# Folding the k and q weights in 64 x 64 tiles, and a stated order of landings for the first loads

## The chip, the cores and the metric

The kernel runs on one core of a Trainium2 chip. The time is device time in microseconds (us) of the whole program; smaller is better. The instructions of a core go to five engines that each work through a queue of their own, in order: TensorE (PE in the profile; its weight loads are shown apart as PEld), VectorE (DVE), ScalarE (ACT), GpSimd (POOL) and SyncE (SP), which here only issues DMA transfers. An engine that has to wait for another one waits on a semaphore, and everything behind the waiting instruction in its queue waits with it.

## The reference

One transformer block on x of 2048 tokens by 640 features, with adaptive layer norm from a condition vector c:

```python
mod = (_silu(c) @ w_mod).reshape(c.shape[0], 6, 1, -1)
sa, ca, ga, sb, cb, gb = (mod[:, 0], mod[:, 1], ...)
h = _layernorm(x, axis=-1) * (1 + ca) + sa
x = x + ga * _A_ref(h, A_wqkv, A_w_phi, A_wo)
h = _layernorm(x, axis=-1) * (1 + cb) + sb
x = x + gb * _B_ref(h, B_w1, B_b1, B_w2, B_b2)
```

`_A_ref` is linear attention with 32 heads of 20 features. Each head's q and k go through that head's own 20 x 20 matrix before two softmaxes:

```python
pq = jnp.einsum("bhsd,hdf->bhsf", q, w_phi)
pk = jnp.einsum("bhsd,hdf->bhsf", k, w_phi)
phi_q = jnp.concatenate([_softmax(pq, axis=-1), _softmax(-pq, axis=-1)], axis=-1)
```

`_B_ref` is an MLP with a squared ReLU. The change touches only the work that comes before the first projection of tokens: `w_phi` is multiplied into the q and k weights once (the folds), the first 256 tokens are normalised, and shift `sa` and scale `ca` are computed from c.

## The kernel before

**Stages.** The kernel has a prologue (lines 149 to 691 of the source below), a loop over 16 blocks of 128 tokens for k, v, q and the attention sums, a second pass that makes the attention output, and the MLP. In the prologue the order of each engine's instructions is the order of the source (`tc.manual_schedule` at line 150 names all five engines).

**The folds.** `fold(nm, d)` at line 265 makes 128 rows (chunk d, of five) of the k or q weights with `w_phi` multiplied in. The raw weights lie transposed: 120 columns, or six heads, on 120 partitions, five such groups side by side in one chunk, and the last 40 columns of all chunks in a small piece of their own (`wk1`, `wq1`). The moving operand `bd_t` is block diagonal: six 20 x 20 blocks of `w_phi` for each group (lines 241 to 251, from the loaded `bd` and the mask `own`). So one fold is six products of 120 x 128 weights with 120 (the last: 40) moving columns, into two PSUM banks. In fp32 a product is two records in the profile, so a fold has 12 records. Then `split()` copies each bank to SBUF, rounded, with ACT and puts the rest beside it with DVE (`lo`, line 91). `pj` is a set of four PSUM banks, so two folds can be under way; the first fold of q uses two of the three `kvp` banks instead.

**The other work of the prologue.** `stats` (line 543) takes mean and variance of the first 256 tokens with DVE and then makes bias and scale of the norm with four small POOL instructions (lines 553 to 556). `scale` (line 559) applies them with ACT. `t_in` (line 354) turns the normalised block with PE, ten transposes into `TR`, halves of the `kvp` banks. `mod_rows2` (line 568) multiplies c into a chunk of the shift and scale weights (`WM`, loaded from `w_ss`), with four 32-column tiles side by side; `mod_sb` copies the result to SBUF with ACT, `mod_cols2` turns it with PE and sums it with DVE into `cols_a`. `out0(d)` applies `cols_a` to chunk d of the turned tokens with ACT twice and DVE once (`t_out`, line 365). `k_step(d)` is the first use of all this: 12 products of the k projection.

**The order on PE** is written out in lines 614 to 655: nine warm-up products, the folds of k's chunks 0 to 3, then of k's chunk 4 and q's chunks 0 to 3, the first `mod_rows2`, the transposes of x, and after them a chain of columns, second `mod_rows2`, q's last fold, third `mod_rows2`, and the five `k_step`. On ACT `scale` stands between the splits of q's chunks 1 and 2; on DVE `stats` stands between the splits of k's chunks 3 and 4.

**The loads.** SP issues them in the order of lines 226 to 239: k's five chunks and small piece, the first block of x, q's chunks 0 to 3, two chunks of `w_ss`, q's chunk 4, the other three of `w_ss`, the second block of x, v's five chunks. A load waits only for its destination, and for the landing of the transfer issued eight before it, whose semaphore it uses again. POOL sets up constants and masks at the start (lines 153 to 199).

Of the kernel before, what the change touches and what calls it, by code (L numbers as in the profile page):

```python
# [11 lines left out]
AF = mybir.ActivationFunctionType  # L12
ALU = mybir.AluOpType
# [41 lines left out]
def kernel(  # L55
# [34 lines left out]
    def lo(out_lo, full, hi, eng=None):  # L90
        (eng or nc.vector).tensor_tensor(out_lo, full, hi.bitcast(F32), op=ALU.subtract)  # L91
# [4 lines left out]
    def over(ap):  # L96
        return ap[:, :, None].to_broadcast([ap.shape[0], ap.shape[1], DH])
# [43 lines left out]
    def tp(name):  # L141
# [17 lines left out]
    nc.gpsimd.affine_select(out=own, in_=own, compare_op=ALU.is_ge, fill=0.0, base=0,  # L159
                            pattern=[[-DH, 6]], channel_multiplier=1)  # L160
    nc.gpsimd.affine_select(out=own, in_=own, compare_op=ALU.is_ge, fill=0.0, base=DH - 1,
                            pattern=[[DH, 6]], channel_multiplier=-1)
# [20 lines left out]
    for v in vt:  # L183
        nc.gpsimd.memset(v[:, :, DH :], 1.0)

    def head_mask(m, n, at):

        nc.gpsimd.memset(m, 1.0)
        nc.gpsimd.affine_select(out=m, in_=m, compare_op=ALU.is_ge, fill=0.0, base=-at,
                                pattern=[[-DH, n]], channel_multiplier=1)  # L190
        nc.gpsimd.affine_select(out=m, in_=m, compare_op=ALU.is_ge, fill=0.0, base=DH - 1 + at,
                                pattern=[[DH, n]], channel_multiplier=-1)

    mtmp = row("s2", "mtmp")
    mask = mask[:, :3]
    for m, t, n in ((mask, mtmp[:120, :3], 3), (mask5, mtmp[:80, :2], 2)):
        head_mask(m, n, 0)
        head_mask(t, n, DH * n)
        nc.gpsimd.tensor_tensor(m, m, t, op=ALU.add)

    nc.scalar.dma_start(bdc[:120, :120], bd)
    nc.scalar.dma_start(c_t, c)
    bd_t = row("s4", "bd_t")
    raw, WM, RV, XB = {}, {}, {}, {}

    def load_raw(nm, w5, w1, ds=range(NC)):
        if 0 in ds:
            raw[nm] = [tok2("w", f"raw_{nm}{i}") for i in range(3)]
            nc.vector.memset(raw[nm][2][:, 1], 0.0)
        for d in ds:  # L210
            nc.sync.dma_start(raw[nm][d // 2][:, d % 2], w5[d * P : (d + 1) * P])
            if d == 0:
                nc.sync.dma_start(raw[nm][2][:40, 1], w1)

    def load_x(j):
        XB[j] = tok2(f"x{j % 2}", f"xb{j}")
        nc.sync.dma_start(XB[j], x[256 * j : 256 * j + 256].rearrange("(i p) d -> p i d", p=P))

    def load_wm(d):
        WM[d] = flat(tok2(("k", "k", "q0", "q1", "w")[d], f"wm_{d}"))  # L220
        nc.sync.dma_start(WM[d], w_ss[d * P : (d + 1) * P])

    def flat(e):
        return e.rearrange("p s d -> p (s d)")

    load_raw("k", wk5, wk1)
    load_x(0)
    load_raw("q", wq5, wq1, range(4))
    for d in range(2):
        load_wm(d)  # L230
    load_raw("q", wq5, wq1, (4,))
    for d in range(2, NC):
        load_wm(d)
    load_x(1)
    for d in range(NC):
        if d % 2 == 0:
            both = tok2("w", f"rawv{d}")
        RV[d] = both[:, d % 2]
        nc.sync.dma_start(RV[d], wv[d * P : (d + 1) * P])

    by_head = bdc[:120, :120].rearrange("p (g f) -> p g f", f=DH)
    for a, b in ((0, 3), (3, 5)):
        nc.vector.tensor_tensor(
            bd_t[:120, 120 * a : 120 * b].rearrange("p (g i f) -> p g i f", i=6, f=DH),
            by_head[:, a:b, None, :].to_broadcast([120, b - a, 6, DH]),
            own[:, None, :, None].to_broadcast([120, b - a, 6, DH]), op=ALU.mult
        )
    nc.vector.tensor_tensor(
        bd_t[:120, 600:].rearrange("p (i f) -> p i f", f=DH),
        by_head[:, 5:6, :].to_broadcast([120, 2, DH]), over(own[:, :2]), op=ALU.mult  # L250
    )

    cs = const.tile([P, NC], F32, name="cs")
# [11 lines left out]
    def fold(nm, d, p=None):  # L265

        w = wslot(f"w{nm}{d}")
        W[nm, d] = w
        p = p or pj(f"fold{nm}{d}")
        for g, (o, n) in enumerate(GR):  # L270
            if g < 5:
                r = raw[nm][d // 2][:120, d % 2, g * P : (g + 1) * P]
            else:
                r = raw[nm][2][:120, 1, d * P : (d + 1) * P]
            nc.tensor.matmul(  # L275
                p[g // 3][:, (g % 3) * 120 : (g % 3) * 120 + n], r, bd_t[:120, g * 120 : g * 120 + n],
                start=True, stop=True,
            )

        def split():  # L280
            for h, (a, b) in enumerate(((0, 360), (360, 640))):
                nc.scalar.activation(w[:, 0, a:b], p[h][:, : b - a], AF.Copy)
                lo(w[:, 1, a:b], p[h][:, : b - a], w[:, 0, a:b])

        return split

# [67 lines left out]
    def t_in(xn, d, p, mixed=False):  # L354
        for i in range(2):
            src = by_turn(xn[:, i])[:, d] if mixed else xn[:, i, d * P : (d + 1) * P]
            nc.tensor.transpose(p[:, i * P : (i + 1) * P], src, ident)  # L357
# [254 lines left out]
        t_out(cols_a, HT[0], d, "a0", TR[d])  # L612

    warm = tp("warm")
    for i in range(WARM):
        nc.tensor.matmul(warm[:, :P], ones, ones, start=True, stop=True)
    for d in range(4):
        fold("k", d)()
    n0 = stats(XB[0], "a0")
    fold("k", 4)()  # L620
    fold("q", 0, kvp[1:])()
    fold("q", 1)()
    scale(XB[0], *n0)
    fold("q", 2)()
    split = fold("q", 3)
    mod_rows2(0)
    mod_sb(0)
    for d in range(NC):
        t_in(XB[0], d, TR[d])
    split()  # L630
    mod_cols2(0)
    out0(0)
    mod_rows2(1)
# [21 lines left out]

    def v_hi(d):
        W["v", d] = wslot(f"wv{d}")
# [1131 lines left out]
```

## Time and profile before

| | us |
|---|---|
| median of three runs | 747.2 |
| lowest, highest | 746.77, 747.63 |
| the profiled execution, its own time | 746.64 |
| its span, from the first to the last instruction | 744.9 |
| PE busy in the span | 738.1 |
| POOL busy in the span | 169.1 |

The granted TensorE clock is 1.0 in the profiled execution. Busy time says how long an engine had work under way, and not whether the work was of use; the chain of waits follows the end of the program back, at each step to what released it. The rows of the prologue stand in the prediction below, where they are used.

### The profile page before, as it was taken

The numbers are of one execution on the slowest core, as the hardware profiler recorded it, in microseconds if no ns is written. First come the engines' busy times: TensorE is split into PE (matmuls) and PEld (weight loads), VectorE is DVE, ScalarE is ACT, GpSimd is POOL, SyncE is SP. The second block draws the span as 40 slices with busy tenths as digits, with TensorE's granted clock in tenths as the row PEclk, the third lists the DMA queues.
The fourth block names the chain that finished last, engine by engine and source line by source line (L and its number), as shares of the span: only waits on it lengthen the run. The fifth ranks groups of instructions, "written<-read, shape, count | busy, mean of one in ns | idle before, by whom it ended". The sixth has DMA issues, their size and how long they took to land.

```text
span 744.9 us, 16612 instructions
## 1 busy us (share of the span) xinstructions
PE 738.1 (99%) x6523; PEld 720.6 (97%) x6523; DVE 598.8 (80%) x1089; ACT 453.1 (61%) x1028; POOL 169.1 (23%) x352
## 2 busy tenths in 40 slices
PE   9999999999999999999999999999999999999997
PEld 9999999999999988998999999999999999999997
DVE  6598988987999999999755777877786776777766
ACT  5767566657863355567687667475574747647431
POOL 2000101001100337547303040231321313222110
PEclk9999999999999999999999999999999999999999
DMA  8812341343331254754885567897667768667461
GB/s 330 339 37 106 111 134 59 107 143 107 126 124 72 83 184 152 173 137 106 209 251 166 154 199 255 271 312 211 180 190 201 214 184 240 187 176 213 129 183 36
DMA packets 58800, 126.46 MB, mean 170 GB/s; under 512 B 7438, under 2 KB 16403, under 8 KB 58723
## 3 DMA queue, kind: packets, MB, share of 16 engines
q1 hardware_dynamic: 38636, 79.20, 32.4%
q0 software_dynamic: 17504, 40.90, 22.1%
q10 hardware_dynamic: 2583, 5.30, 1.9%
q8 instruction: 51, 0.84, 0.5%
q14 instruction: 26, 0.21, 0.1%
HBM read 100.74 MB, written 29.89 MB: 175 GB/s over the span
## 4 chain that ended last, share of the span: by engine, by line
PE 88%; DVE 6%; ACT 3%; POOL 1%; issue 1%; ACTq 0%; DVEq 0%; POOLq 0%
PE up L81 25%; PE acc L81 18%; PE pk L81 8%; PE pwo L81 8%; PE pv L81 8%; PE pq L81 6%; PE acc3x L81 5%; PE te L943 2%; PE kvp L448 1%; DVE dn L875 1%; PE foldk L275 1%; PE numa L81 1%; PE ta L357 1%; DVE scr L873 1%; PE foldq L275 1%
## 5 line engine op out<-in xcount | busy, mean ns | idle before, releaser
L81 PE MATMUL up<-h,w 128*128 128x256 f32 x1640 | 204.6, 276 | 0.1
L81 PEld LDWEIGHTS up<-h,w 128*128 128x128 f32 x1640 | 196.5, 188 | 0.7 <-DVE h L91 0.5
L1338 ACT ACTIVATE ft<-up,b_t 128x256 f32<-128x256 f32 x104 | 49.2, 473 | 95.6 <-PE up L81 95.2
L81 PE MATMUL acc<-w,ra 128*128 128x384 f32 x452 | 97.5, 335 | 0.0
L1339 DVE TENSOR_TENSOR ft<-ft 128x256 f32<-128x256 f32 x104 | 43.8, 421 | 43.0 <-ACT ft L1338 41.5
L81 PE MATMUL pwo<-wo,ot 128*128 128x384 f32 (+1 forms) x480 | 78.1, 313 | 0.0
L81 PE MATMUL pq<-wq,hT 128*128 128x384 f32 (+1 forms) x480 | 75.8, 312 | 0.0
L81 PEld LDWEIGHTS acc<-w,ra 128*128 128x128 f32 x452 | 72.7, 188 | 0.8 <-DVE ra L91 0.6
L81 PE MATMUL pk<-wk,hT 128*128 128x384 f32 (+1 forms) x480 | 73.1, 309 | 0.0
L81 PE MATMUL pv<-wv,hT 128*128 128x380 f32 (+1 forms) x480 | 73.0, 309 | 0.0
L81 PEld LDWEIGHTS pwo<-wo,ot 128*128 128x128 f32 x480 | 69.5, 188 | 2.8 <-issue 2.7
L81 PEld LDWEIGHTS pq<-wq,hT 128*128 128x128 f32 x480 | 71.3, 188 | 0.7 <-issue 0.5
L81 PEld LDWEIGHTS pv<-wv,hT 128*128 128x128 f32 x480 | 71.3, 188 | 0.0
L81 PEld LDWEIGHTS pk<-wk,hT 128*128 128x128 f32 x480 | 70.8, 188 | 0.5 <-ACT hT L369 0.2
L91 DVE TENSOR_TENSOR ra<-ft,ra 128x384 fp32r<-128x384 f32 (+2 forms) x86 | 36.8, 448 | 32.6 <-ACT ra L1362 18.8
L1448 POOL DMA_DIRECT2D ring_a<-td_a x34 | 18.5, 543 | 117.2 <-PE acc L81 103.5
L1362 ACT ACTIVATE ra<-ft 128x384 fp32r<-128x384 f32 x48 | 25.2, 526 | 28.4 <-DVE ft L1339 22.3
L81 PE MATMUL acc3x<-w,ra 128*128 128x256 f32 x231 | 39.5, 278 | 0.0
L81 PEld LDWEIGHTS acc3x<-w,ra 128*128 128x128 f32 x231 | 37.2, 188 | 0.0
L439 DVE TENSOR_REDUCE sk<-ek 128x64 f32<-128x1280 f32 x16 | 23.7, 1482 | 15.1 <-ACT ek L434 10.7
L1353 DVE TENSOR_TENSOR ft<-ft 128x128 f32<-128x128 f32 x136 | 33.3, 286 | 1.2
L334 POOL TENSOR_SCALAR sma<-sma 128x2 f32<-128x2 f32 x6 | 3.1, 516 | 134.9 <-ACT xb L333 134.9
(255 smaller groups left out, 1442.5 us busy)
## 6 DMA issues: line engine op xcount, KB each, us to landing
ring_c<-td_c POOLq DMA_DIRECT2D x34, 384.0 KB, 4.0
ring_a<-td_a POOLq DMA_DIRECT2D x34, 384.0 KB, 3.4
ring_b<-td_b POOLq DMA_DIRECT2D x34, 256.0 KB, 3.6
esp<-eq SPq DMA_DIRECT2D x12, 640.0 KB
el<-esp SPq DMA_DIRECT2D x12, 640.0 KB
rw<-in_w SPq DMA_DIRECT2D x23, 320.0 KB
wm<-in_w_mod SPq DMA_DIRECT2D x20, 320.0 KB
xb<-in_x SPq DMA_DIRECT2D x8, 640.0 KB
```

What stands on the lines that cost most here:

```text
L81: nc.tensor.matmul(o, a, b, start=first and i == 0, stop=last and i == len(terms) - 1, skip_group_check=skip,)
L91: (eng or nc.vector).tensor_tensor(out_lo, full, hi.bitcast(F32), op=ALU.subtract)
L275: nc.tensor.matmul(p[g // 3][:, (g % 3) * 120 : (g % 3) * 120 + n], r, bd_t[:120, g * 120 : g * 120 + n], start=True, stop=True,)
L357: nc.tensor.transpose(p[:, i * P : (i + 1) * P], src, ident)
L439: nc.vector.tensor_reduce(s, heads(flat(e)), axis=AX.X, op=ALU.add)
L448: nc.tensor.matmul(kvp[0][32 * c : 32 * c + DH + 1, a - g % 3 * DH : a - g % 3 * DH + 2 * m].rearrange("p (s n) -> p s n", s=2)[:, :, h % ...
L943: nc.tensor.transpose(p[:124, a : a + P], EU[2 * j + i][:, 2 * g + c, :124], ident)
L1338: nc.scalar.activation(r, p, AF.Relu, bias=b1_t[:, f : f + 1])
L1339: nc.vector.tensor_tensor(r, r, r, op=ALU.mult)
L1353: nc.vector.tensor_tensor(t[:, o], t[:, a], t[:, b], op=op)
L1362: nc.scalar.activation(a[:, 0, :3], t[:, :3], AF.Copy)
L1448: nc.gpsimd.dma_start(RING[j, n, r], TD[n][r].bitcast(F32R))
```

## The change

It has four parts.

1. **The folds.** Columns of the raw weights are dealt to two halves of the partitions: the first 16 heads to partitions 0 to 59, the other 16 to 64 to 123, 60 columns (three heads) a group, five groups, and the last 20 columns of each half in the small piece. A fold is then six groups of four products, each of a 64 x 64 tile of the raw weights with 60 (the last: 20) moving columns. The two row halves go to the two PSUM banks, the two column halves to the two halves of a bank's partitions. `bd` and `own` follow (the mask of three heads for each half), `bd_t` is made by one DVE instruction, and the splits are cut at 320 columns instead of 360.
2. **The loads.** `load` can be given the landed tile of another load. Then POOL copies one element of that tile into the first element of the destination, and SP's issue waits for the copy. The loads after k's wait so: x's first block for k's chunk 1, q's chunks 0 and 1 for k's chunks 3 and 4, and so on, as written below. Their order on SP is the same. The small pieces are loaded as two halves each. The last nine loads are written behind `stats`, in `loads1()`.
3. **The order.** q's chunk 3 is split before the first `mod_rows2`, and the transposes of x stand before that `mod_rows2`, not behind it. The constant columns of `vt` and the masks are made on POOL after `scale` of the second block.
4. **The warm-up** has three products with 384 moving columns in place of nine with 128.

```diff
+FOLDS = [(60 * g, 60) for g in range(5)] + [(300, DH)]
...
-    own = bdc[:120, P : P + 6]
-    nc.gpsimd.memset(own, 1.0)
...
+    own6 = bdc[:, 120:126]
+    own = own6[:, :3]
+    nc.gpsimd.memset(own6, 1.0)
...
+    nc.gpsimd.tensor_tensor(own, own, own6[:, 3:], op=ALU.add)
...
-    for m, t, n in ((mask, mtmp[:120, :3], 3), (mask5, mtmp[:80, :2], 2)):
-        head_mask(m, n, 0)
-        head_mask(t, n, DH * n)
-        nc.gpsimd.tensor_tensor(m, m, t, op=ALU.add)
...
+    def masks():
+        for v in vt:
+            nc.gpsimd.memset(v[:, :, DH :], 1.0)
+        for m, t, n in ((mask, mtmp[:120, :3], 3), (mask5, mtmp[:80, :2], 2)):
+            head_mask(m, n, 0)
+            head_mask(t, n, DH * n)
+            nc.gpsimd.tensor_tensor(m, m, t, op=ALU.add)
...
+    def head(ap):
+        return ap[:1, :1]
+
+    def load(to, of, after=None):
+        if after is not None:
+            nc.gpsimd.tensor_copy(head(to if len(to.shape) == 2 else to[:, 0]), head(after))
+        nc.sync.dma_start(to, of)
...
+    for d in range(NC):
+        load_raw("k", wk5, wk1, d)
+    k_, q_ = (lambda d: chunk("k", d)), (lambda d: chunk("q", d))
+    load_x(0, k_(1))
+    load_raw("q", wq5, wq1, 0, k_(3))
+    load_raw("q", wq5, wq1, 1, k_(4))
+    load_raw("q", wq5, wq1, 2, XB[0][:, 0])
+    load_raw("q", wq5, wq1, 3, XB[0][:, 0])
+    load_wm(0, q_(0))
+    load_wm(1, q_(2))
+    load_raw("q", wq5, wq1, 4, q_(3))
+
+    def loads1():
+        load_wm(2, WM[0])
+        load_wm(3, WM[1])
+        load_wm(4, q_(4))
+        load_x(1, WM[2])
+        load_v(0, WM[3])
+        load_v(1, WM[4])
+        load_v(2, XB[1][:, 0])
+        load_v(3, XB[1][:, 0])
+        load_v(4, RV[0])
...
-        for g, (o, n) in enumerate(GR):
-            if g < 5:
-                r = raw[nm][d // 2][:120, d % 2, g * P : (g + 1) * P]
-            else:
-                r = raw[nm][2][:120, 1, d * P : (d + 1) * P]
-            nc.tensor.matmul(
-                p[g // 3][:, (g % 3) * 120 : (g % 3) * 120 + n], r, bd_t[:120, g * 120 : g * 120 + n],
-                start=True, stop=True,
-            )
+        for g, (o, n) in enumerate(FOLDS):
+            r = raw[nm][d // 2][:, d % 2, g * P : (g + 1) * P] if g < 5 else raw[nm][2][:, 1, d * P : (d + 1) * P]
+            for a in (0, 64):
+                for c in (0, 64):
+                    nc.tensor.matmul(
+                        p[a // 64][c : c + 64, o : o + n], r[a : a + 64, c : c + 64], bd_t[a : a + 64, o : o + n],
+                        start=(g == 0), stop=True, skip_group_check=True,
+                    )
...
-    for i in range(WARM):
-        nc.tensor.matmul(warm[:, :P], ones, ones, start=True, stop=True)
+    for i in range(WARM // 3):
+        nc.tensor.matmul(warm[:, : 3 * P].rearrange("p (a n) -> p a n", a=3), ones, ones[:, None, :].to_broadcast([P, 3, P]), start=True, stop=True)
     for d in range(4):
         fold("k", d)()
     n0 = stats(XB[0], "a0")
+    loads1()
     fold("k", 4)()
     fold("q", 0, kvp[1:])()
     fold("q", 1)()
     scale(XB[0], *n0)
     fold("q", 2)()
-    split = fold("q", 3)
+    fold("q", 3)()
+    for d in range(NC):
+        t_in(XB[0], d, TR[d])
     mod_rows2(0)
     mod_sb(0)
-    for d in range(NC):
-        t_in(XB[0], d, TR[d])
-    split()
     mod_cols2(0)
     out0(0)
     mod_rows2(1)
...
         if d == 3:
             scale(XB[1], *n1)
+            masks()
```

More of the change, by code (lines that the diff above doesn't have):

```diff
@@ L204, with chunk, load_raw, load_x @@
     raw, WM, RV, XB = {}, {}, {}, {}
[L206 to L215, printed above, removed]
-        XB[j] = tok2(f"x{j % 2}", f"xb{j}")
[L217 to L221, printed above, removed]
+    def head(ap):
[4 more added lines that the diff above has]
+        nc.sync.dma_start(to, of)
+    def chunk(nm, d):
+        return raw[nm][d // 2][:, d % 2]
+    def load_raw(nm, w5, w1, d, after=None):
+        load(chunk(nm, d), w5[d * P : (d + 1) * P], after)
+        if d == 0:
+            for a in range(2):
+                nc.sync.dma_start(raw[nm][2][64 * a : 64 * a + DH, 1], w1[DH * a : DH * a + DH])
+    def load_x(j, after=None):
+        XB[j] = tok2(f"x{j % 2}", f"xb{j}")
+        load(XB[j], x[256 * j : 256 * j + 256].rearrange("(i p) d -> p i d", p=P), after)
+    def load_wm(d, after=None):
+        load(WM[d], w_ss[d * P : (d + 1) * P], after)
+    def load_v(d, after=None):
+        load(RV[d], wv[d * P : (d + 1) * P], after)
     def flat(e):
         return e.rearrange("p s d -> p (s d)")
[L226 to L234, printed above, removed]
+    for nm in "kq":
+        raw[nm] = [tok2("w", f"raw_{nm}{i}") for i in range(3)]
+        nc.vector.memset(raw[nm][2][:, 1], 0.0)
+    for d in range(NC):
+        WM[d] = flat(tok2(("k", "k", "q0", "q1", "w")[d], f"wm_{d}"))
     for d in range(NC):
@@ L624 @@
     fold("q", 2)()
-    split = fold("q", 3)
+    fold("q", 3)()
+    for d in range(NC):
+        t_in(XB[0], d, TR[d])
     mod_rows2(0)
     mod_sb(0)
-    for d in range(NC):
-        t_in(XB[0], d, TR[d])
-    split()
     mod_cols2(0)
```

46 lines of the change are left out of this document (20 added, 26 removed).

## The prediction

> **What bounds the kernel now.** I read the page first, then the chain of waits, the windows with their transfers, SP's own waits, and last the timeline of the first 40 us, where the whole change lies.
>
> ```profile
> PE 738.1 (99%) x6523; PEld 720.6 (97%) x6523; DVE 598.8 (80%) x1089; ACT 453.1 (61%) x1028; POOL 169.1 (23%) x352
> ```
>
> The page leaves 6.8 us of a 744.9 us span in which PE does nothing. A delay of PE in the prologue therefore reaches the end in full, and so does a gain, if PE is really let go earlier. The chain of waits through the prologue (start, us, what):
>
> ```profile
> 1.05 4.21 PE warm L616 x18
> 5.26 6.80 PE foldk L275 x60
> 12.06 1.34 PE kvp L275 x12
> 13.40 4.02 PE foldq L275 x36
> 17.41 0.78 PE mrow L577 x20
> 18.19 1.24 PE kvp L357 x10
> ...
> 20.32 1.46 PE foldq L275 x12
> ```
>
> PE alone is on it. The ten folds cost 6.80 + 1.34 + 4.02 + 1.46 = 13.6 us, 1.34 each. Halved, they would give back 6.7 us, which is the gain that the chain offers. But a chain shows who came last, not who came a moment before. The windows show the transfers (us, busy time of each engine, clock, DMA share, GB/s):
>
> ```profile
> 0.00:5.00 5.00, 3.95 (x18) 3.95 (x19) 1.93 (x4) 1.28 (x1) 3.47 (x27) 1.00 0.58 162
> 5.00:10.00 5.00, 5.00 (x45) 5.00 (x44) 3.39 (x11) 3.03 (x8) 0.52 (x3) 1.00 0.99 360
> 10.00:15.00 5.00, 5.00 (x47) 5.00 (x47) 4.58 (x13) 3.32 (x8) 1.08 (x3) 1.00 1.04 412
> ```
>
> From 5 us on the DMA engines are full too. When single loads landed is read from SP, whose issues wait for earlier landings. First SP's timeline between 11 and 14.6 us (the first line began before), then what SP waited for in it (total us, times, longest):
>
> ```profile
> 10.83 0.33 SPq L211 DMA_DIRECT2D raw_q<-in_wq  x1
> 11.64 1.52 SPq L221 DMA_DIRECT2D wm<-in_w_ss  x3
> 13.67 0.38 SPq L217 DMA_DIRECT2D xb<-in_x  x1
> 14.49 0.33 SPq L239 DMA_DIRECT2D rawv<-in_wv  x1
> ```
>
> ```profile
> SPq L211 <- DMA xb<-in_x: 1.6, 1, 1.6
> SPq L221 <- DMA raw_q<-in_wq: 1.0, 3, 0.5
> SPq L217 <- DMA raw_q<-in_wq: 0.5, 1, 0.5
> SPq L239 <- DMA raw_q<-in_wq: 0.4, 1, 0.4
> ```
>
> So x's first block landed just before 10.83, and the five raw_q loads issued by then (chunk 0, the small piece, chunks 1 to 3) just before 11.64, before the next issue, before 12.83 (11.64 + 1.52 less one issue of 0.33), before 13.67 and before 14.49: a landing of a chunk every 0.8 us. PE began q's first fold at 12.06, 0.4 us after chunk 0 was there, and its fourth, after 13.40 + 2 x 1.34, at 16.1. Faster folds up to here run into the landings; what they make room for is 1 or 2 us, not 6.7.
>
> **The change part by part.** *The folds.* Six products, 12 records with their weight loads, took 1.34 us, so 0.112 us a record, and ten 128-column transposes took 1.24, so 0.124 with the switch between shapes. 120 columns would stream in less than they took; the load of 128 weight columns sets the 0.112. A new record loads 64 columns, 0.056 us if in proportion (an estimate), and 48 of them in four lots side by side make 12 x 0.056 = 0.67 us a fold. Two rows bear on "side by side": 32-column tiles (chain of waits) and tiles of 21 rows with 240 to 360 columns to stream (timeline).
>
> ```profile
> 60.77 1.41 PE kvp L448 x125
> 247.92 0.87 PE L811 MATMUL z<-kvs,ident 21*128 21x360 f32 x8
> ```
>
> 125 records in 1.41 us is 11 ns each; and eight z records in a row would need 2.5 us by the transposes' rate (320 columns on average, 0.3 us each), and took 0.87. Column tiles and row tiles do overlap. The ends: 48 x 0.011 = 0.53 us, and 48 x 0.056 = 2.7 us if the combination did not overlap; I take 0.67.
>
> The Trainium skill, page "TensorE: Matmul & The Clock Gate", section "Wait — 56ns, not 53.3ns?", says that starts of matmuls never come closer than about 25 ns. By it a fold would be 48 x 25 ns = 1.2 us (an estimate), hardly a gain. The 11 ns of the row above speak against it where tiles lie side by side.
>
> *The splits* stay (two ACT and two DVE instructions a fold), cut at 320 instead of 360 columns: nothing. *bd_t* becomes one DVE instruction in place of three: nothing, since warm-up covers it.
>
> *The gates.* Seventeen loads now have a one-element POOL copy before them that reads a landed tile and writes the next one's first element; SP's issue waits for the copy. POOL works in order, and so does SP. Before stats' POOL work on x's first block stand eight copies, and the last of them, for q's chunk 4, reads q's chunk 3. That is the point of this forecast. The rows of before:
>
> ```profile
> 3.77 0.19 POOL L199 TENSOR_TENSOR mask<-mask,mtmp 120x3 f32<-120x3 f32 x1
> 11.55 0.88 DVE L551 BATCH_NORM_STATS2 sta<-xb 128x6 f32<-128x320 f32 x2
> 13.76 0.24 POOL L553 TENSOR_SCALAR sqa<-mva 128x2 f32<-128x2 f32 x1 [8.08 <-DVE mva L552]
> 14.17 1.01 ACT L282 ACTIVATE wq<-foldq 128x360 fp32r<-128x360 f32 x2 [0.33 <-PE foldq L275]
> 14.34 0.88 DVE L91 TENSOR_TENSOR wq<-kvp,wq 128x360 fp32r<-128x360 f32 x2
> 15.43 1.73 ACT L561 ACTIVATE xb<-xb,nba,sqa 128x640 f32<-128x640 f32 x2 [0.25 <-POOL nba L556]
> 17.34 0.85 PE L577 MATMUL mrow<-wm,cs 128*32 128x128 f32 x20
> 18.12 1.31 PE L357 MATMUL kvp<-ident,xb 128*128 128x128 f32 x10
> 18.24 0.37 ACT L585 ACTIVATE msb<-mrow,plus 128x128 f32<-128x128 f32 x1 [0.44 <-PE mrow L577]
> 19.81 0.15 DVE L592 TENSOR_REDUCE cols_a<-kvp 128x2 f32<-128x4 f32 x1
> 20.00 0.56 ACT L368 ACTIVATE hfa<-kvp,cols_a 128x256 f32<-128x256 f32 x1 [0.73 <-DVE cols_a L592]
> 20.92 0.35 ACT L585 ACTIVATE msb<-mrow,plus 128x128 f32<-128x128 f32 x1
> 21.61 0.31 PE L590 MATMUL kvp<-ident,msb 128*128 128x128 f32 x1
> 22.63 2.00 PE L81 MATMUL pk<-wk,hT 128*128 128x384 f32 x12
> ```
>
> Step by step. Chunk 3 lands at 14.5, as before: the bytes ahead of it are the same. The copy, by the nearest row (0.19), is done at 14.7. From the first of the four POOL instructions to the scaling is 15.43 - 13.76 = 1.67: 16.4. Scaling x, 1.73: 18.1, against 17.16. PE's transposes of x now stand ahead of the first row products (mod_rows2), and all but the first wait for the second half of x: they start at 18.15 and the products, 1.25 later, at 19.4 (18.12 to 19.48 before, less one transpose). Products 0.85: 20.25; by then ACT has split q's chunks 2 and 3 (two pairs of 0.9 to 1.0 from 18.1). Copy to SBUF 0.05 + 0.37: 20.7. Transpose 0.31 and reduce 0.15, with their starts 0.5: 21.2. hfa and hT, 20.00 to 20.92 before with the sum's second half beside them, 1.0: 22.25. The next copy, 0.35: 22.6, and only then the second transpose, 22.65. From it to k's first product was 22.63 - 21.61 = 1.02: 23.67, against 22.63. **The sum is 1.04 us later.** The faster fold of q's chunk 4 lies inside: it starts about 21.7 and ends by 22.4, before the second transpose can begin; at 1.34 it would add 0.4.
>
> In before, the first row products (17.34) ran while x was being scaled. That cover is gone: they now come after the transposes and before the copy that the columns wait for, and the split of q's chunk 3, which before stood behind that copy, is ahead of it on ACT. After k's first product all keeps its order. The fourth and fifth row products, behind k's first product, need the last w_ss chunk. Its landing shows in an issue of SP and its wait:
>
> ```profile
> 23.49 0.33 SPq L499 DMA_DIRECT2D bb<-in_b  x1
> ```
>
> ```profile
> SPq L499 <- DMA wm<-in_w_ss: 1.3, 1, 1.3
> ```
>
> It is there at 23.5; PE came for it at 22.63 + 2.00 = 24.6 and would now come at 25.7: no bound.
>
> *The transfers behind the gates.* One isolated load shows what a gate costs when the queue is empty (windows as above, load issued at 39.00, 0.66 MB):
>
> ```profile
> 39.00:40.00 1.00, 1.00 (x8) 1.00 (x7) 0.96 (x2) 0.97 (x3) 0.00 (x0) 1.00 0.00 0
> 40.00:41.00 1.00, 1.00 (x7) 1.00 (x6) 1.00 (x2) 0.53 (x2) 0.00 (x0) 1.00 0.88 131
> ```
>
> A microsecond passes without a byte, and the next one runs at 131 instead of 412 GB/s, 0.7 us lost: 1.7 in all. Each gate opens two or more loads ahead: chunks q2 and q3 are issued when x lands (10.8 + 0.3), with q0 and q1 still to come until 12.8, so 1.7 us lie in the queue, just what is needed. I take nothing lost, with 0.5 earlier and 1.5 later as ends. The small pieces go as two loads each: one issue more on SP, 0.4 us at most, ahead of k's chunk 1; nothing, by the 162 GB/s that the first 5 us reach anyway.
>
> *The masks* go behind the second block's statistics on POOL. They keep a buffer that the second k tile needs, so ACT may wait some 0.3 us near 34 us; PE does not need that copy until its second q tile near 39 us. Nothing.
>
> **The rivals.**
> 1. *The gate on POOL is harmless*, because chunk 3 lands well before 14.5. Then the statistics set the scale: DVE could begin them at 10.9, be done at 13.1 (11.55 to 13.76 before), POOL at 14.8. But q's fourth fold needs PSUM that DVE frees at 15.7 (13.1 and three pairs of 0.88), so PE ends it at 16.4, comes to x at some 16.6 and to the products 1.36 later, at 18.0: 1.4 off the 1.04, **-0.4 us, 746.8**.
> 2. *Faster: the loads gain from less crowding.* The first 5 us moved 162 GB/s and the next 360, from a first issue at
>
> ```profile
> 0.80 0.38 SPq L211 DMA_DIRECT2D raw_k<-in_wk  x1
> ```
>
>    At 412 from 1.8 us on, a microsecond after it, all landings would come 1.2 + 0.6 = 1.8 us sooner, and with rival 1: **-2.2, 745.0**. For it: the loss lies where SP issues without pause. Against it: k's five loads are still issued together.
> 3. *Slower: the queue runs dry at a gate*, q2 and q3 above all. One dry gate costs up to 1.7 us, straight into chunk 3's landing: at 1.5, **749.7**. It decides from 0.5 on.
> 4. *The clock falls.* The warm-up took 4.21/18 = 0.234 us for 128 columns, the transposes 0.124: PE began at half speed. PE would stand idle for half of 5 to 18 us (nine folds of 0.67 are 6.0), by the landings never over 2 us in one piece. If it fell back for as long as at the start, 4.2 us at half speed cost 2.1: **750.3**. The Trainium skill, same page, section "What's actually happening", puts the half clock behind an idle window of about 3.4 us. By that rule it stays up here; no idle of PE in this trace tests it.
> 5. *The tiles do not overlap*, so the change isn't what it says: nine folds of 2.7 us from 5.3 on end at 29.6 instead of 17.4, **759**.
>
> **How the numbers follow.** The forecast has 0.40, the rivals 0.14, 0.15, 0.21, 0.07 and 0.03. The sum made against the profiled execution (746.64) gives 747.7; that run lies 0.56 under the median of 747.2, so for the median I add the same 1.0: **748.2 us**. About 0.2%, 1.5 us, is what a measurement here can tell from no change: forecast and rival 1 lie within it, 0.54; faster 0.15; slower 0.31. The range leaves out rival 5, the far half of rivals 2 and 4 and some of 3: 745.2 to 750.3. The likeliest case's own range is 747.5 to 748.7.
>
> **What would show it.** Right: a fold of some 0.67 us in the chain, gaps of PE before q's folds, the first POOL instruction of stats released just after q's chunk 3 lands and not by DVE, x scaled near 18 us, k's first product near 23.7. Wrong: POOL's statistics waiting for DVE (rival 1 or 2), a window between 8 and 18 us well under 400 GB/s (rival 3), folds or transposes at twice their time behind a gap (rival 4), folds of 2 us (rival 5). A different order of ACT and DVE after 60 us, which a scheduler arranges, would be outside of all this.

## The result, and the profile after

The changed kernel takes 753.69 us (median of four runs, 752.42 to 753.86) where the kernel before, on the same chip, took 747.03. The ratio is 1.0084, with a 95% interval of 1.0067 to 1.0102: slower by 6.7 us, and outside the range that was given. The profiled execution took 753.78, its span 752.1.

The page of the kernel after, its line of busy times and the line of PE's instruction queue (packets, MB, share), to which the text comes back below:

```profile
PE 737.7 (98%) x6871; PEld 716.7 (95%) x6871; DVE 598.2 (80%) x1087; ACT 451.6 (60%) x1028; POOL 174.8 (23%) x370
...
q8 instruction: 54, 0.88, 0.5%
```

PE is idle for 14.4 us of the span, 7.6 more than before. The chain of waits through the prologue (start, us, what) says for what:

```profile
2.37 4.64 DMA raw_k<-in_wk
...
7.27 4.69 DMA xb<-in_x
...
12.72 4.67 DMA raw_q<-in_wq
...
17.72 4.90 DMA raw_q<-in_wq
...
22.87 8.52 DMA wm<-in_w_ss
...
31.52 0.92 PE mrow L603 x20
...
40.02 4.42 PE pq L82 x30
```

In before this stretch was PE alone, up to the first step of the q projection:

```profile
33.52 4.31 PE pq L81 x30
```

Now five transfers stand one behind the other, with a POOL copy between each two: 7.01, 11.96, 17.40, 22.62, 31.39 are the landings of k's chunk 1, x, q's chunks 3 and 4, and the last chunk of `w_ss`. The q projection starts at 40.02 instead of 33.52. These 6.50 us are nearly the whole loss, and this start serves below as the measure of the prologue (set against the medians, the later stages add or give back 1 or 2 us from run to run, in e12 and e3 some 3, which wasn't followed up).

The windows (us, busy time of each engine with its records, clock, DMA share, GB/s), at the places of those of before:

```profile
5.00:10.00 5.00, 4.17 (x189) 3.57 (x192) 2.96 (x10) 2.36 (x7) 0.52 (x3) 1.00 0.93 322
10.00:15.00 5.00, 1.72 (x82) 1.46 (x74) 3.92 (x11) 1.53 (x4) 0.46 (x3) 0.79 0.84 281
15.00:20.00 5.00, 3.71 (x138) 3.53 (x137) 1.78 (x4) 2.07 (x5) 1.74 (x6) 0.50 0.97 334
20.00:25.00 5.00, 4.53 (x93) 4.05 (x87) 1.68 (x4) 2.86 (x7) 0.52 (x3) 0.69 0.89 273
```

The last two windows of before, whose first ones stand in the prediction:

```profile
15.00:20.00 5.00, 5.00 (x72) 4.58 (x72) 2.85 (x8) 3.58 (x9) 0.30 (x2) 1.00 1.02 406
20.00:25.00 5.00, 5.00 (x68) 4.33 (x64) 1.97 (x6) 3.32 (x9) 0.00 (x0) 1.00 1.03 402
```

Two things are new: the transfers run at 273 to 334 GB/s where before ran at 360 to 412, and the granted clock is half from 12.87 to 23.11. The timeline of the same stretch (start, us, engine, line, operation; in brackets the idle time before it and what ended it):

```profile
14.62 1.49 PE L301 MATMUL kvp<-bd_t,raw_q 64*64 64x60 f32 x48 [3.28 <-DMA raw_q<-in_wq]
18.96 2.74 PE L301 MATMUL foldq<-bd_t,raw_q 64*64 64x60 f32 x90 [1.29 <-issue]
23.57 0.85 PE L603 MATMUL mrow<-wm,cs 128*32 128x128 f32 x20
27.81 2.00 PE L82 MATMUL pk<-wk,hT 128*128 128x384 f32 x12
...
17.52 0.17 POOL L216 COPY raw_q<-raw_q 1x1 f32<-1x1 f32 x1 [0.59 <-DMA raw_q<-in_wq]
17.78 0.24 POOL L579 TENSOR_SCALAR sqa<-mva 128x2 f32<-128x2 f32 x1
```

PE's second stop is marked "issue": the profile shows nothing that it waited for. That mark turned out to be half of the story.

### The profile page after: what moved, and what is told of

It is laid out like the page before. It is cut to its first block, busy times and chain, and to the rows that moved or that the text cites. A ratio compares the mean times of both kernels' runs of the same rounds, so it can differ in the third digit from the quotient of the medians.

```text
span 752.1 us, 17358 instructions
## 1 busy us (share of the span) xinstructions
PE 737.7 (98%) x6871; PEld 716.7 (95%) x6871; DVE 598.2 (80%) x1087; ACT 451.6 (60%) x1028; POOL 174.8 (23%) x370
## 4 chain that ended last, share of the span: by engine, by line
PE 83%; DVE 6%; ACT 4%; DMA 4%; POOL 1%; issue 1%; SPq 0%; ACTq 0%; POOLq 0%; DVEq 0%
PE up L82 25%; PE acc L82 18%; PE pk L82 8%; PE pv L82 8%; PE pwo L82 8%; PE pq L82 6%; PE acc3x L82 5%; PE te L970 2%; DMA raw_q<-in_wq 1%; DMA wm<-in_w_ss 1%; DVE dn L902 1%; PE kvp L474 1%; PE numa L82 1%; PE ta L383 1%; DVE scr L900 1%
```

## The experiments

Two theories stood at the start: **G**, the gates cost transfer rate, and **C**, the half clock costs. The first four runs (e1 to e4) added **F**, that the folds in 64 x 64 tiles cost by themselves, by something that the profile files under "issue", and **B**, that two bias loads (0.33 MB) cost. "Their order on SP is the same", as the list of the change has it, does not hold for these two: in before SP issues them behind v's loads, in the kernel after the small one (7 KB) ahead of x at 4.85 and the large one (320 KB) at 7.69, behind x and ahead of q; in e2 both stand ahead of x. Each run was timed beside the kernel before on the same chip: 747.57 us for e1 to e4, 748.65 for e5 to e8, 748.83 for e9 to e11, 748.96 for e12.

### Each half of the change alone

**e1_no_gates** is the kernel after without the copies:

```diff
     def load(to, of, after=None):
-        if after is not None:
-            nc.gpsimd.tensor_copy(head(to if len(to.shape) == 2 else to[:, 0]), head(after))
         nc.sync.dma_start(to, of)
```

> The kernel after with all seventeen one-element copies taken out, so that the loads are issued as in the kernel before, eight ahead; folds, order on PE and masks as after. Theory G (the gates starve the transfers: k's first product came at 27.8 us instead of 22.6, the last w_ss chunk landed at 31.4 instead of 23.5): landings as before, q's chunk 3 near 14.5 and the last w_ss chunk near 23.5 us, time 746.5 to 748. Rival C (the clock, which fell to half from 12.9 to 23.1 us because faster folds leave PE idle): the clock falls here too, k's first product after 25 us, time 749 or more. Rival S (another order of ACT and DVE in later stages): time near 753 with the prologue as before.

Measured: 752.19, ratio 1.0062 (1.0046 to 1.0077). The loads land nearly as in before: the last chunk of `w_ss` is there when SP issues the load behind it, at 24.81, where before has 23.49 and the kernel after 31.39. The loss stays. Its chain:

```profile
10.71 2.68 issue
13.39 0.85 PE foldk L299 x25
...
17.07 2.48 issue
```

PE stops twice for over 2 us without a releaser, both times in the middle of a fold. So "G and nothing else" falls.

**e2_gates_alone** is the kernel before with the copies, the order of loads of the change and `loads1()`, and its own 120 x 128 folds:

```diff
+    def load(to, of, after=None):
+        if after is not None:
+            nc.gpsimd.tensor_copy(head(to if len(to.shape) == 2 else to[:, 0]), head(after))
+        nc.sync.dma_start(to, of)
...
+    load_x(0, k_(1))
+    load_raw("q", wq5, wq1, 0, k_(3))
...
     n0 = stats(XB[0], "a0")
+    loads1()
```

> The kernel before with the gates alone: the copies on POOL and the loads behind them, folds of 120 columns, masks and order on PE as before. Theory G: late as the kernel after, 752 to 755, last w_ss chunk after 29 us. Rival C: PE is busier by twice the folds, so the clock holds, and the time is under 750. Rival S: 747 to 748.

Measured: 752.94, ratio 1.0069 (1.0046 to 1.0091); clock 1.0, no stop by "issue". Two of its windows, and two groups of row products in its timeline:

```profile
15.00:20.00 5.00, 4.63 (x56) 4.55 (x56) 2.15 (x6) 2.50 (x5) 1.91 (x7) 1.00 0.98 313
20.00:25.00 5.00, 4.44 (x53) 3.41 (x46) 2.78 (x8) 3.97 (x11) 0.36 (x3) 1.00 0.91 305
```

```profile
25.00 0.85 PE L604 MATMUL mrow<-wm,cs 128*32 128x128 f32 x20 [0.54 <-DMA wm<-in_w_ss]
...
29.01 0.85 PE L604 MATMUL mrow<-wm,cs 128*32 128x128 f32 x20 [0.31 <-DMA wm<-in_w_ss]
```

313 and 305 GB/s where before had 406 and 402, and the row products wait for `w_ss`. So each half alone costs some 5 us, and both together 6.7, not 10: the two costs lie over each other.

### The gates: which loads, and how deep

**e6_biases_behind** is e2 with the two bias loads written behind v's, which takes them out of the way of x and q:

```diff
         load_v(4, RV[0])
+        nc.sync.dma_start(b1_t, b1)
+        nc.sync.dma_start(bb, bass.AP(tensor=b2.tensor, offset=b2.offset, ap=[[0, P], [1, D]]))
```

> The gates alone (as in the run of that name), but the two bias loads (b1, b2) that SP took in between k's last chunk and x are written behind v's loads, where they were before. Theory G (the gates starve the transfers): at most 1.5 us better than the gates alone, still 750 to 753, transfers near 300 GB/s between 8 and 30 us. Rival B (the 0.33 MB of biases ahead of x and q is what comes late): 747 to 749.

Measured: 752.1, ratio 1.0054 (1.0034 to 1.0073); q starts at 37.97 instead of 39.05. Theory B has 1 us of e2's delay; the other 4.5 stay.

**e7_gates_deeper** is e6 with each gate on a load some five places ahead instead of two or three:

```diff
-    load_x(0, k_(1))
-    load_raw("q", wq5, wq1, 0, k_(3))
+    load_x(0)
+    load_raw("q", wq5, wq1, 0, k_(0))
...
-        load_wm(2, WM[0])
+        load_wm(2, q_(1))
```

> As the run before, biases behind, but each gate opened earlier: x's first block free, q's chunk 0 for k's chunk 0, and so on, every load behind the landing of the one some five loads ahead instead of two or three. Theory G: with five loads in the queue the rate comes back to 400 GB/s and the time to 746.5 to 749. Rival H (each copy on POOL and each wait on SP costs time by itself, however early): 750 to 753.

Measured: 748.68, ratio 1.0006 (0.9995 to 1.0017), the same time as before. The windows (10 to 25 us):

```profile
10.00:15.00 5.00, 5.00 (x47) 5.00 (x46) 4.44 (x12) 3.14 (x9) 0.69 (x4) 1.00 1.05 403
15.00:20.00 5.00, 5.00 (x60) 4.75 (x59) 2.90 (x8) 4.18 (x9) 1.90 (x9) 1.00 0.98 345
20.00:25.00 5.00, 5.00 (x67) 4.31 (x66) 2.30 (x8) 3.39 (x9) 0.53 (x3) 1.00 1.00 407
```

The rate is mostly back, 378 GB/s over the stretch from 5 to 25 us where before has 395 and e6 has 294, with sixteen of the seventeen copies still there. It is not the copies on POOL that cost, nor SP's waits, but how little stands in the queues while they last. Theory G holds. (Why the engines' share stays at 0.8 to 0.97 while less is moved is not shown.)

### The folds: what "issue" is

**e4_folds_alone** is the kernel before with the new layout, the 64 x 64 folds and the wide warm-up, no gates:

```diff
...
+            for a in (0, 64):
+                for c in (0, 64):
+                    nc.tensor.matmul(
+                        p[a // 64][c : c + 64, o : o + n], r[a : a + 64, c : c + 64], bd_t[a : a + 64, o : o + n],
+                        start=(g == 0), stop=True, skip_group_check=True,
+                    )
...
```

> The kernel before with the 64 x 64 folds alone (with their new layout, split loads of the small pieces, and the warm-up of three wide products): no gates, masks first, first row products ahead of the transposes of x. Theory G: the loads set the pace, so the faster folds bring little: 745.5 to 747.5. Rival C: the clock falls between 10 and 20 us, 749 or more. Rival S: near 753.

Measured: 752.78, ratio 1.0068 (1.0051 to 1.0086). Its chain, cut to the stops and what follows each:

```profile
10.62 2.42 issue
13.04 0.85 PE foldk L301 x25
...
16.43 2.78 issue
19.21 2.54 PE foldq L301 x65
...
24.75 0.50 issue
25.25 0.64 PE mrow L603 x14
```

6.5 us of stops with the one at 30.89 (0.79), against 6.1 by which q is late. (Faster folds give something back, and two stretches of 3.41 us at half clock take something; how much each is was not separated here, see e12.) Where PE stops shows in windows cut at the stops (second column PE, third PEld, with their records in brackets):

```profile
0.00:10.50 10.50, 8.73 (x221) 5.89 (x222) 4.83 (x13) 4.47 (x11) 4.22 (x30) 1.00 0.77 245
...
13.00:16.30 3.30, 3.26 (x127) 3.25 (x127) 2.29 (x7) 1.53 (x4) 1.40 (x4) 0.55 1.04 402
```

Between two stops lie 127 + 127 records and two semaphore instructions of PE, which a window doesn't count: 256. With these counted, 449 instructions of PE lie ahead of the first stop, 705 ahead of the second, 961 ahead of the third. In e1 the first two stand at the same counts, and the stop of the kernel after that was marked "issue" (18.96) stands at 705. The pages name who deals in such lots. q8 moved 54 packets of 16 KB in the kernel after (its line stands above); the line of before:

```profile
q8 instruction: 51, 0.84, 0.5%
```

51 x 256 = 13,056, and PE and PEld of before have 2 x 6523 = 13,046 records; 54 x 256 = 13,824, and after has 2 x 6871 = 13,742 (with PE's semaphore instructions 13,139 and 13,838). A packet of q8 is one block of 256 PE instructions, by these counts. (The Trainium skill, page "Runtime: NRT & Kernel Launch", section "Instruction fetch mechanics", says that instructions are refilled in blocks of 16 KiB, 256 instructions, while the block before runs, and that this is mostly hidden. The size agrees with these rows. That it is hidden does not, here.) In the first stop of e4, 10.5 to 13 us, the queues moved (packets, MB, share):

```profile
q1 hardware_dynamic: 359, 0.78, 103.0%
q8 instruction: 1, 0.02, 2.5%
```

The block is on its way while PE stands, through DMA engines that are full with loads: it starts at 10.79, 0.17 after the stop began, takes 1.0, and PE goes on 1.26 after its end. PE had begun the 256 instructions that end at this stop at 7.39, so 3.40 us passed before the next packet moved; in the kernel after, with less in the queues, it was 0.59 (7.64 to 8.23). From one restart of e4 to the next are 19.21 - 13.04 = 6.17 and 25.25 - 19.21 = 6.04 us. So in this stretch one block arrives in some 6 us, and PE stands still where it uses one up in less. A fold of before has 24 records, weight loads included, in 1.34 us: a block lasts 14 us. A 64 x 64 fold has 96 in some 0.8: a block lasts 2.

**e8_warm_nine** is e4 with nine narrow warm-up products, 24 records more ahead of the folds (a single run, so no interval):

```diff
-    for i in range(WARM // 3):
-        nc.tensor.matmul(warm[:, : 3 * P].rearrange("p (a n) -> p a n", a=3), ones, ones[:, None, :].to_broadcast([P, 3, P]), start=True, stop=True)
+    for i in range(WARM):
+        nc.tensor.matmul(warm[:, :P], ones, ones, start=True, stop=True)
```

> The folds alone with the old warm-up of nine narrow products, so 12 records or 24 instructions more ahead of the first fold, in the same time. Theory F: PE's gaps stand before the same instructions 449 and 705 counted from the program's start, so 12 records earlier in k's chunk 4 and in q's chunk 2 than with the wide warm-up; lengths 2 to 3 us as before. Rival T: the gaps stay at the same record of the same fold.

Measured: 753.74. The window up to the first stop:

```profile
0.00:10.60 10.60, 8.36 (x221) 7.68 (x222) 4.87 (x13) 4.50 (x11) 4.12 (x30) 1.00 0.78 244
```

The same 221 + 222 records as in e4, though 36 of them are warm-up now, weight loads included, and 12 were in e4. The stop (2.47 us, from 10.71) has moved to an earlier place in the folds with them. It is a place in the stream of instructions, and no operand, that PE waits for.

**e5_row_tiles** halves the number of products, row tiles of 64 x 128:

```diff
-                for c in (0, 64):
-                    nc.tensor.matmul(
-                        p[a // 64][c : c + 64, o : o + n], r[a : a + 64, c : c + 64], bd_t[a : a + 64, o : o + n],
+                nc.tensor.matmul(
+                    p[a // 64][:, o : o + n], r[a : a + 64], bd_t[a : a + 64, o : o + n],
```

> The folds alone (as in the run of that name), but each fold with two tiles of 64 rows and 128 columns in place of four of 64 x 64: 24 records a fold instead of 48, so half as many instructions on PE. Theory F (PE runs out of instructions: in the two runs without gates it stands still before its instruction 449, 705, 961 and 1217, always 256 apart, for 2.6 and 3.0 us at the first two, with a 16 KB packet of the instruction queue inside the gap, and the clock falls behind it): 256 instructions last twice as long, so the gaps shrink to under 1 us each, the clock stays up, time 746 to 749. Rival T (tiles of 64 rows as such, by a change of shape or by the clock, bring the loss): 751 to 753.

Measured: 759.1, ratio 1.0148 (1.0103 to 1.0193). The stops are gone as theory F has it, and yet this is the slowest kernel of all. Its windows:

```profile
9.40:14.00 4.60, 4.60 (x48) 4.60 (x46) 2.08 (x6) 1.53 (x4) 0.00 (x0) 0.50 1.03 352
14.00:19.00 5.00, 5.00 (x51) 5.00 (x50) 3.48 (x11) 1.53 (x4) 1.40 (x4) 0.50 1.02 406
```

PE has work in every instant, and the clock is half (until 29.87). So the clock has a condition other than idle time.

**e9_row_tiles_twice** is e5 with each product's columns streamed twice, the second time into PSUM that nothing reads:

```diff
...
-                    p[a // 64][:, o : o + n], r[a : a + 64], bd_t[a : a + 64, o : o + n],
+                    bass.AP(tensor=t.tensor, offset=t.offset, ap=[t.ap[0], [far, 2], [1, n]]),
+                    r[a : a + 64], m[:, None, :].to_broadcast([64, 2, n]),
```

> The folds in row tiles of 64x128 (twelve products a fold), each product streaming its 60 columns twice, the second copy into PSUM columns that nothing reads; no gates, loads in the order of before. The number of instructions is that of the run with row tiles, whose clock was half from 9.39 to 29.87 us though PE had no stop. Theory A (a clock window is judged by the share of the time in which columns stream, not by stops between records): a product streams 120 columns, 0.05 us at full clock, against the 0.11 us that its weights take, about as much as a product of before, so the clock stays at 1.0 in all windows after its rise, a fold is 1.3 to 1.4 us, pq starts at 33 to 34 us, and the time is 747 to 749.5. Rival R (the switch of tile shape or position itself holds the clock down, however much is streamed): clock 0.5 again over the folds, 2.3 us or more a fold, pq at 40 us or later, 755 or more. Both expect no stop of PE at an instruction count, as in the run with row tiles.

Measured: 750.52, ratio 1.0029 (1.0017 to 1.0041), 1.0 over the expected 747 to 749.5; q at 35.27. Its windows at the places of e5's:

```profile
9.40:14.00 4.60, 4.60 (x84) 4.52 (x82) 3.51 (x9) 2.56 (x7) 0.00 (x0) 1.00 1.04 361
14.00:19.00 5.00, 5.00 (x85) 4.83 (x83) 3.45 (x11) 3.64 (x9) 1.40 (x4) 1.00 1.03 408
```

Twice the columns, 8.6 us faster, as the clock is full. (Of the 1.75 us by which q is still late, 1.1 are there when q's first fold begins, at 13.2 instead of 12.06; the loads of this layout land later too, the last chunk of `w_ss` by 24.9 instead of 23.5. The cause of that wasn't tested.) The expectation gave a wrong price for a column, though. In e3 (below) ten records, which are five fp32 products of 384 columns, take 3.42 us at full clock:

```profile
11.43 3.42 PE warm L645 x10
```

That is 0.89 ns a column in each record, so 120 columns stream for 0.107 us. From that price the use of the array by a fold, as a share of its rows and of the time, can be estimated: in before 2 x 640 columns, 1.14 us, on 120 of 128 rows in 1.34 us, 80%; in e9 2 x 1,280 columns on half of the rows, 1.14 of 1.34, 85%; in e5 half of that work in no less time (1.45 us for its last fold, at full clock), about 40%. The clock goes with this share, and a rule of time with any column streaming can't be told from it here.

**e12_four_twice** is e4 with columns streamed twice, to part the stops from the clock:

```diff
...
-                        p[a // 64][c : c + 64, o : o + n], r[a : a + 64, c : c + 64], bd_t[a : a + 64, o : o + n],
+                        bass.AP(tensor=t.tensor, offset=t.offset, ap=[t.ap[0], [far, 2], [1, n]]),
+                        r[a : a + 64, c : c + 64], m[:, None, :].to_broadcast([64, 2, n]),
```

> All ten folds in tiles of 64x64 (24 products each) without gates, each product streaming its 60 columns twice, the second copy into PSUM columns that nothing reads; the instructions are as many as in the run with the folds alone. Theory F (the stops are set by the count of instructions and cost the time by themselves): PE stops again ahead of its 449th and its 705th instruction, for 2 to 3 us each less what its slower folds give back, whatever the clock does, and pq starts 4 to 6 us later than in the kernel before: 751 to 754. Rival K (it is the clock that costs, since too few columns stream in the 64x64 tiles): with twice the columns the clock stays at 1.0 outside the stops, the folds end as early as before, and the time is 747 to 749.5.

Measured: 752.68, ratio 1.0051 (1.0032 to 1.0071). The clock is half in one window only (15.2 to 18.6), and the stops remain, shorter since the folds are slower:

```profile
11.81 2.12 issue
...
18.82 1.18 issue
...
24.90 1.24 issue
```

q starts at 39.98, 6.5 late. The stops are 4.5 us of it; 3.4 us at half clock can cost 1.7 at most. Rival K falls as the main cause: the stops cost by themselves.

**e11_k_in_four** has k's folds in 64 x 64 tiles and q's in row tiles with columns streamed twice:

```diff
+            for a in (0, 64) if nm == "k" else ():
+                for c in (0, 64):
...
+            for a in (0, 64) if nm == "q" else ():
+                t, m = p[a // 64][:, o : o + n], bd_t[a : a + 64, o : o + n]
```

> No gates; k's five folds in tiles of 64x64 (24 products each), q's five in row tiles of 64x128 with their 60 columns streamed twice (12 products each). Theory F: the 449th PE instruction falls at the end of k's folds, so one stop of 2 to 3 us stands there, at 10.5 to 13.2 us, which the landing of q's first chunk (13.06 in the run without gates) covers; the 705th comes only some 60 products later, in q's folds, 5 us after, at half the rate of instructions, so its block has landed or the stop is under 1 us; pq starts at 33.5 to 35.5 us and the time is 747 to 750. Rival (the stops come from the tiles of 64x64 themselves, not from the count): none but in k's folds, and the same time; rival R (tile shape lowers the clock): clock 0.5 through q's folds and 752 or more.

Measured: 752.84, ratio 1.0059 (1.0040 to 1.0078): missed. The stop is there, alone, as expected, but it outlasts the landing of q's first chunk, which is there by 12.61 (SP's next issue waited for it):

```profile
10.82 2.69 issue
13.51 0.85 PE foldk L301 x25
14.35 2.71 PE kvp L308 x24
17.07 5.53 PE foldq L308 x70
```

q's first fold starts at 14.35, 1.1 later than in e9, whose folds of q are the same. And it takes 2.71 us: the clock is half from 12.87 to 19.70. Of the 3.5 us by which q's projection starts later than in e9 (38.80 and 35.27), 1.1 are the part of the stop that was not covered, and the other 2.4 come with the half clock. Rival R also expected 752 or more; its reason, the tile shape, is excluded by e9, where the same folds of q run at full clock.

### The clock, and the loads, in the kernel after

**e3_pe_kept_busy** is the kernel after with eight products of 384 columns that nothing reads, between the folds:

```diff
+    def keep(n):
+        for _ in range(n):
+            nc.tensor.matmul(warm[:, : 3 * P].rearrange("p (a n) -> p a n", a=3), ones, ones[:, None, :].to_broadcast([P, 3, P]), start=True, stop=True)
```

> The kernel after with eight products of 384 columns without use set between the folds where PE stood idle (five before q's chunk 0, one each after q's chunks 1, 2 and 3), so that the clock does not fall. Theory G: the clock stays at 1.0, and yet the last w_ss chunk lands near 31 us and the time is 753 to 754. Rival C: 750 or less.

Measured: 757.73, ratio 1.0142 (1.0122 to 1.0163), over what either theory expected. The clock is half for one window (18.97 to 22.38) instead of three, and q starts at 40.27, no earlier than in after. But this run can't tell the theories apart: the last `w_ss` is there by 30.10, when POOL's copy reads it, PE comes to its row products only at 31.33, and the eight added products took 6.7 us of PE's time. What does tell is the chain of the kernel after: from 2.37 to 31.39 it has loads, their issues and the copies, and nothing of PE, so PE at full clock would have waited for the same landing. In the kernel after the clock costs nothing that the loads don't cost already. Why e3 ends 4 us behind the kernel after, nearly all of it later than the prologue, wasn't followed up.

**e10_folds_gates_deeper** has the 64 x 64 folds with the deep gates of e7:

```diff
+    load_x(0)
+    load_raw("q", wq5, wq1, 0, k_(0))
...
+                        p[a // 64][c : c + 64, o : o + n], r[a : a + 64, c : c + 64], bd_t[a : a + 64, o : o + n],
```

> The folds in tiles of 64x64 of the change, with the gates of the run that cost nothing (each load waits for one some five places ahead, the biases behind v's loads). Theory F (PE takes instructions in blocks of 256 faster than the packets that bring them get through the load queues) with theory G (shallow gates cost transfer rate): the rate is about 400 GB/s, the last chunk of w_ss has landed by 24.5 to 26 us, and PE stands still ahead of its 449th or 705th instruction, or both, with stops of 1 to 3 us each, shorter than the 2.6 and 3.0 without gates as the queues are five deep at most; the time is 749.5 to 753. Rival G alone (all that the change costs is the shallow gates): no stop over 1 us, pq at 33 to 34 us, 747 to 749.

Measured: 754.83, ratio 1.0086 (1.0062 to 1.0111), 1.8 over the expected 749.5 to 753. The transfers are back at 400 GB/s (407 and 405 between 15 and 25 us), and the chain has the stops:

```profile
10.47 3.44 issue
...
17.12 2.36 issue
```

They are no shorter than without gates, the clock is half from 14.64 to 24.88, and q starts at 39.08. Mending the gates alone lets q start 0.9 earlier than in the kernel after and brings no time that can be told from none. All in one table (time; how much longer than the kernel before on the same chip; in brackets the start of q's projection):

| folds | no gates | gates 2 or 3 ahead | gates 5 ahead |
|---|---|---|---|
| 120 x 128 tiles | before, 747.0 (33.5) | e2, 752.9, +5.4 (39.1) | e7, 748.7, 0.0 (34.3) |
| 64 x 64 tiles | e1, 752.2, +4.6 (40.3) | after, 753.7, +6.7 (40.0) | e10, 754.8, +6.0 (39.1) |

None of the kernels beats the one before.

## Why the prediction failed, step by step

**The bound.** That the first folds can't run past the landings held, and the folds' own price came near: 0.82 us for the last fold of e4, where 0.67 was forecast, against 1.46 in before. The reason given for the 0.112 us a record is in doubt: by e3's price 120 columns stream for 0.107, nearly all of it, and no run shows that the load of 128 weight columns sets it.

**The gates on POOL.** Right as a mechanism. The statistics start at 17.78, right behind the copy at 17.52 that reads q's chunk 3 (landed 17.40), and not when DVE is done, so rival 1 is out. From the first row product to k's first product it is 27.81 - 23.57 = 4.24 us; 4.27 were forecast. So of the 5.2 us by which k's first product is late, 1.04 are the forecast's own sum and 2.9 the later landing; the other 1.2 came ahead of the row products, where folds and transposes ran at half clock (the transposes 2.00 us instead of 1.31). The masks and the splits stand on no step of the chain, as said.

**The transfers behind the gates** is the step that failed: "I take nothing lost, with 0.5 earlier and 1.5 later as ends." q's chunk 3 landed at 17.4 and not at 14.5, the last `w_ss` chunk at 31.4 and not at 23.5: 2.9 and 7.9 us. I had priced one gate, and asked whether a queue runs dry there. It does not run dry for long: the share of the DMA engines is 0.84 to 0.97. It runs thin, at about 300 GB/s for as long as the gates last, and every load behind them inherits that. "No bound" for the fourth and fifth row products fell by the same error: they wait for `w_ss` and add some 1.3 us to the 5.2 by which k's first product is late. Rival 3 pointed the right way, with the price of one gate in place of all. Beyond that the bias loads, whose move ahead the prediction does not price, cost 1 us where both stand ahead of x and q (e2 against e6); in the kernel after the large one stands behind x, and what it costs there wasn't measured. The "nothing" for the small pieces in halves is not borne out either: without gates the new layout's last `w_ss` chunk lands by 24.8 (e1) and 24.9 (e9), 1.3 us or more later than in before, and which part of the layout does it stays open.

**The folds.** "Inside", hence free, was the second failure, hidden in after behind the first. The forecast counted 48 records a fold as time on the array, and not as instructions that must be fetched. e4 prices the folds with their layout at 5.2 us alone, and e10 shows that it would have come up as soon as the gates were mended.

**The clock.** Rival 4 had 0.07, on the ground that PE is never idle for long in one piece. The longest stop was 3.28 us and came from a landing, and the clock fell 1.5 us after it began (11.34 to 12.87). In after it cost nothing beyond the loads, by the chain; in e11 it is 2.4 us. The rule that the prediction set beside it (the Trainium skill, page "TensorE: Matmul & The Clock Gate", section "What's actually happening": half clock behind an idle window of about 3.4 us) has the right grain, for the half-clock stretches here are 3.41 us long or multiples of it. But the window need not be idle: in e4 the clock fell 1.9 us into a stop of 2.42, and in e5 with no stop at all.

**The tiles overlap** (rival 5 is out): six groups of four products, 48 records and as many weight loads, took 0.82 us. (The floor of about 25 ns between starts of matmuls, which the prediction quotes from the same page of the Trainium skill, would make 1.2 us of it; across tiles that lie side by side it doesn't hold.)

## What to carry to other kernels

Before cutting an operation into smaller ones, count its instructions as traffic: find the queue that brings them, see how long one block takes under the load that the stage has, and ask whether the new instructions use a block up faster. Before holding loads back by a chain of landings, ask how many bytes stand in the queues at each moment, not whether a queue runs dry at one gate. A stage with two limits close together (landings and PE here) must be tested with each of them mended alone and both together, since either one alone shows nothing.

## What the runs showed of the hardware

- PE's instructions come in blocks of 256 through the same DMA engines as the loads. With those full, a block took some 6 us from the restart before it (e4); PE then stood for 0.4 to 3.4 us at several block ends between 10 and 33 us. In the kernel after, whose gates keep the queues short, the first block came at 8.23 instead of 10.79, and the first stop is missing (7.5 to 10.4 us, packets, MB, share):

```profile
q8 instruction: 1, 0.02, 2.7%
```

- The granted clock fell to half with PE's records back to back, where the work filled about 40% of the array by the estimate above (e5), and stayed full with 85% (e9).
- Gates two or three loads deep held the transfers at 294 GB/s between 5 and 25 us, gates five deep at 378 (e6 and e7; before 395), with nearly the same copies on POOL.
- A stop can cost more afterwards than while it lasts: in e11 1.1 us of a stop of 2.69 were not covered by a landing, and the half clock of 6.83 us that began during it cost 2.4.
